# One fused attention, expert and token-mixing kernel on one core: the same instructions in another order

## The chip, the cores and the metric

The kernel runs on one core of one Trainium2 chip. The metric is the device time of one execution in microseconds (us). The kernel before took 493.33 us, the median of 3 runs (492.98 to 493.48). The engines are called as in the profile: PE (TensorE matmuls), PEld (its weight loads), DVE (VectorE), ACT (ScalarE), POOL (GpSimd), SP (the queue that issues most DMAs).

## What is computed

The reference chains three layers. Batch is 2, heads 8, sequence 768, head width 64, model width 512.

```python
q_bucket = bits of (q @ proj > 0); k_bucket likewise
mask     = q_bucket[:, :, :, None] == k_bucket[:, :, None, :]
scores   = where(mask, q @ k.T / 8, -1e9);  x = softmax(scores) @ v

for e in range(4):                      # causal attention per expert, weight of the top 2
    a = softmax(causal(x @ wq[e] @ (x @ wk[e]).T / 8)); ye = a @ (x @ wv[e]) @ wo[e]
    out += w[:, :, e] * ye

theta = x @ w_theta
y = w_tok_r @ (x * cos(theta)) + w_tok_i @ (x * sin(theta));  u = x + y
return u + relu(u @ w_ch)
```

## The kernel before

**First stage, 0 to about 240 us: hashed attention.** Sixteen heads, six row tiles of 128 queries each. A `Unit` is one such tile of a head against all 768 keys, and passes through these steps:

- `scores`: four matmuls (L986) on PE into a PSUM tile `ps`, of which there are three.
- `low`: DVE scales and masks them, with the row minimum (L1007), into the SBUF tile `T`. This frees the `ps` tile.
- `exp` on ACT (L1015).
- `flip`: DVE transposes `T` in blocks of 32 (L1022). In every second head one of the six units goes another way: six PE transposes (L1026) into a `ps` tile and a copy back on ACT (L1035).
- `mix`: when all six units of a head are flipped, a block of 96 small fp32 matmuls (L1060, two passes each, written to `ps` and to two tiles `O`) multiplies with the values `V`; six matmuls at L1068 follow in every second head. The block is held together in the order.
- `gather`, `scale`, `finish_x` on ACT, POOL and DVE end a head pair (L1095 to L1107, L906 to L913, L932).

Beside it run the preparation of later heads: `hash` (L1248, DVE L1251), `split` and `pack` (casts at L739 and L747, bit rows moved by DMA at L1262), the loads of q, k and `V` (L1134, L1140, L1151), and early parts of the later stages: expert projections (L1381, L1318), the product of two weights (`fuse_mm`, L1532, added up on DVE at L1537), and reloads of expert operands (`unstash`, L1407 and L743).

**Second stage, to about 327 us:** the causal expert attention (L1082 is its mix). **Third stage, to the end:** `theta` and `out_proj` (L1585), `trig`, `split_z`, the token mix (L1671) and the channel product (L1600).

The start of the program has a routine of its own (`first_head`): q and k of the first head arrive in pieces, on SP's queue (k, L1134) and ACT's (q, L1140), PE computes the hash bits (L1189, L1198, L1199), and DVE turns them into signs (L1211).

**What sets the order.** The program is written twice. In the first pass every job is recorded in a fixed order, which the lists `LP`, `M0`, `WT` and `VALA` place. `Plan` then replays the recording with a cost for each instruction (`price`), dependencies, PSUM and SBUF buffers, DMA lanes, and a rule for PE's own instruction fetches (`FETCH`): at each step the engine takes the ready instruction with the lowest rank. Ranks come from a backward replay; `NUDGES` then shifts some of them. In the second pass `fix` pins this order on every engine (PE, DVE, ACT, POOL and SP), and each engine works in order.

```python
        part, first, more, wake, gap, took = FETCH
...
                while count >= first + part * len(ends):
                    ends.append(max(at + wake, ends[-1] + gap if ends else 0.0) + took)
...
        for seed, a, b, ns in nudges:
            here = (rank >= a * 1e3) & (rank < b * 1e3)
            if ns < 0:
                here &= scatter(len(rank), seed + 1) > 0.85
            rank = np.where(here, rank + ns * scatter(len(rank), seed), rank)
```

## Time and profile before

| what | value |
|---|---|
| runs | 493.33 us median of 3, 492.98 to 493.48 |
| the profiled execution | 493.23 us, of which the span of the trace is 491.40 us |
| mean granted TensorE clock | 0.997 of full speed |
| busy: PE, PEld, DVE, ACT, POOL | 95%, 76%, 79%, 67%, 59% of the span |
| chain that ended last | PE 72%, DVE 10%, ACT 7%, issue 4%, POOL 3%, DMA 2% |

Busy shares are averages over stages with different limits, and a busy PE is not PE at its peak. "issue" in a chain or behind an idle time means that the engine waited for nothing that the profile names.

### The profile page before, as it was taken

The numbers are of one execution on the slowest core, as the hardware profiler recorded it, in microseconds if no ns is written. First come the engines' busy times: TensorE is split into PE (matmuls) and PEld (weight loads), VectorE is DVE, ScalarE is ACT, GpSimd is POOL, SyncE is SP. The second block draws the span as 40 slices with busy tenths as digits, with TensorE's granted clock in tenths as the row PEclk, the third lists the DMA queues.
The fourth block names the chain that finished last, engine by engine and source line by source line (L and its number), as shares of the span: only waits on it lengthen the run. The fifth ranks groups of instructions, "written<-read, shape, count | busy, mean of one in ns | idle before, by whom it ended". The sixth has DMA issues, their size and how long they took to land.

```text
span 491.4 us, 13377 instructions
## 1 busy us (share of the span) xinstructions
PE 465.1 (95%) x5360; PEld 374.0 (76%) x5360; DVE 386.3 (79%) x668; ACT 329.6 (67%) x658; POOL 288.5 (59%) x243
## 2 busy tenths in 40 slices
PE   8889988989999999898999999999999999999997
PEld 3576866677898777676789877778888888878886
DVE  6999999688894999896677684849869999676543
ACT  7788867586454978869767689997667666571110
POOL 6997999888248479226920046058557697874000
PEclk9999999899999999999999999999999999999999
DMA  7544535445785545873448324512443445470542
GB/s 245 175 140 135 162 120 157 116 149 166 195 301 174 173 151 155 232 254 108 134 150 238 99 75 134 187 38 55 145 144 131 148 151 151 109 209 34 168 145 85
DMA packets 44249, 74.17 MB, mean 151 GB/s; under 512 B 6948, under 2 KB 13892, under 8 KB 44188
## 3 DMA queue, kind: packets, MB, share of 16 engines
q1 hardware_dynamic: 42028, 69.80, 46.4%
q10 hardware_dynamic: 2160, 3.52, 1.9%
q8 instruction: 42, 0.69, 0.6%
q14 instruction: 19, 0.16, 0.1%
HBM read 54.52 MB, written 15.91 MB: 143 GB/s over the span
## 4 chain that ended last, share of the span: by engine, by line
PE 72%; DVE 10%; ACT 7%; issue 4%; POOL 3%; DMA 2%; DVEq 0%; POOLq 0%; ACTq 0%
PE ps L1671 19%; PE ps L986 9%; PE ps L1060 9%; PE ps L1381 6%; PE wk L1585 5%; DVE T L1007 5%; PE wk L1600 4%; PE O L1060 4%; PE ps L1318 4%; PE ps L1026 4%; PE O L1082 3%; PE ps L1600 3%; ACT T L1015 3%; DVE T L1022 3%; PE ps L1068 1%
## 5 line engine op out<-in xcount | busy, mean ns | idle before, releaser
L1015 ACT ACTIVATE T<-T,m 128x768 f32<-128x768 f32 (+3 forms) x144 | 121.2, 844 | 31.8 <-DVE T L1007 31.2
L1007 DVE TENSOR_SCALAR_CACHE_REDUCE T<-ps 128x768 f32<-128x768 f32 (+3 forms) x144 | 115.5, 834 | 32.2 <-PE ps L991 15.0
L1022 DVE STREAM_TRANSPOSE T<-T 128x768 f32<-128x768 f32 x88 | 82.5, 960 | 5.5 <-ACT T L1015 5.1
L1671 PE MATMUL ps<-zh,tok 128*128 128x512 f32 x240 | 76.7, 390 | 0.0
L1060 PE MATMUL ps<-T,V 32*64 32x160 f32 (+1 forms) x1536 | 63.9, 312 | 8.4 <-DVE T L1007 3.3
L1060 PE MATMUL O<-T,V 32*64 32x160 f32 (+1 forms) x1536 | 65.0, 312 | 4.8 <-issue 4.7
L1060 PEld LDWEIGHTS ps<-T,V 32*64 32x64 f32 x1536 | 54.7, 131 | 13.9 <-issue 5.2
L986 PE MATMUL ps<-op 128*128 128x512 f32 (+5 forms) x256 | 60.1, 343 | 1.1 <-DVE op L1211 0.9
L1060 PEld LDWEIGHTS O<-T,V 32*64 32x64 f32 x1536 | 50.1, 131 | 6.4 <-issue 6.3
L1671 PEld LDWEIGHTS ps<-zh,tok 128*128 128x128 f32 x240 | 45.1, 188 | 9.7
L1671 PE MATMUL ps<-zl,tok 128*128 128x512 f32 x120 | 46.3, 391 | 0.0
L802 POOL TENSOR_TENSOR tok<-raw,tok 128x512 fp32r<-128x512 f32 x27 | 41.6, 1550 | 7.9 <-PE ps L1671 4.3
L986 PEld LDWEIGHTS ps<-op 128*128 128x128 f32 (+1 forms) x256 | 39.3, 191 | 8.4 <-issue 2.7
L1035 ACT COPY T<-ps 128x768 f32<-128x768 f32 (+2 forms) x36 | 28.6, 798 | 9.0 <-PE ps L1026 8.5
L739 POOL TENSOR_SCALAR op<-op 64x768 fp32r<-64x768 f32 x8 | 6.8, 853 | 45.6 <-ACT op L1397 28.7
L1026 PE MATMUL ps<-ident,T 128*128 128x128 f32 x216 | 30.7, 277 | 1.8 <-ACT T L1015 1.1
L1107 POOL TENSOR_TENSOR ob<-ob,W 64x768 f32<-64x768 f32 x16 | 29.4, 1835 | 1.3
L1026 PEld LDWEIGHTS ps<-ident,T 128*128 128x128 f32 x216 | 23.7, 141 | 5.8 <-ACT T L1015 2.5
L1015 ACT ACTIVATION_READ_ACCUMULATOR T<-T,m 128x1 f32 x144 | 27.2, 189 | 0.0
L1671 PEld LDWEIGHTS ps<-zl,tok 128*128 128x128 f32 x120 | 22.5, 188 | 4.9
L986 PE MATMUL ps<-op,sql 128*128 128x512 f32 x84 | 24.2, 366 | 2.1 <-DVE T L1007 1.1
L1620 POOL TENSOR_TENSOR kk<-kk,x 128x512 f32<-128x512 f32 x12 | 17.8, 1482 | 13.3 <-ACT kk L1619 13.3
(236 smaller groups left out, 1161.6 us busy)
## 6 DMA issues: line engine op xcount, KB each, us to landing
V<-in_vP_dram SPq DMA_DIRECT2D x48, 256.0 KB
raw<-in_wtok_dram SPq DMA_DIRECT2D x36, 256.0 KB
raw<-tok_d SPq DMA_DIRECT2D x27, 256.0 KB
tok_d<-g SPq DMA_DIRECT2D x18, 256.0 KB
rT<-r_d SPq DMA_DIRECT2D x22, 192.0 KB
qk_d<-op SPq DMA_DIRECT2D x8, 384.0 KB
op<-qk_d SPq DMA_DIRECT2D x8, 384.0 KB
out_dram<-o ACTq DMA_DIRECT2D x11, 256.0 KB
```

What stands on the lines that cost most here:

```text
L802: nc.gpsimd.tensor_sub(l, raw, f(h))
L986: one = nc.tensor.matmul(self.sp[:, c0:c1], lhs, rhs[:, c0 - off:c1 - off], start=a == 0, stop=last)
L1007: i = nc.vector.tensor_scalar(self.ss[:, off:off + w], self.sp[:, off:off + w], -0.125, NEG, op0=OP.mult, op1=OP.min, accum_out=m)
L1015: e = nc.scalar.activation(self.ss[:, off:off + w], self.ss[:, off:off + w], AF.Exp, bias=m, scale=-1.0, accum_out=self.grp.den[:, side, i ...
L1022: nc.vector.transpose(self.ss, self.ss)
L1026: nc.tensor.transpose(self.pt[:, j * 128:(j + 1) * 128], self.P[:, j, :], ident)
L1035: nc.scalar.copy(self.P, src)
L1060: together(nc.tensor.matmul(o[a][half * 64:half * 64 + 64, 0:nb * 32], V[band, n // 4, (n - a) % 4], T[band, 0:nb, n * 32:n * 32 + 32], st ...
L1107: nc.gpsimd.tensor_add(g.ob[keep], g.ob[keep], W[keep])
L1381: nc.tensor.matmul(pp[:, c0:c1], lhs[:, kd, e, :], rhs[kd][:, c0:c1], start=n == 0, stop=n == 3 * NK - 1)
L1600: nc.tensor.matmul(o, lhs[:, sl], rhs[:, kd, cols], start=n == 0, stop=n == 3 * NK - 1)
L1671: nc.tensor.matmul(yp[t], lhs[:, a, t, :], rhs[:, a], start=i == 0 and a == 0 and n == 0, stop=i == NT - 1 and a == 1 and n == 2)
```

## The change

All of it is in the constants at the head of the file. The code, and with it every instruction, is the same.

```diff
-LP = [0, 4.5, 5.5, 2.5, 8.5, 6, 9, 13, 10, 15.0, 17.5, 15]
+LP = [0, 4.5, 5.5, 2.5, 8.5, 6, 9, 11, 10, 15.0, 17.5, 15]
-M0 = [4.5, 6, 5.5, 6, 7, 8.0, 9, 11, 11, 11, 13, 14, 12, 12, 14]
+M0 = [4.5, 6, 5.5, 6.5, 7, 8.0, 9, 11, 11, 11, 13, 14, 12, 12, 14]
-WT = [52, 51.0, 57, 52.5]
+WT = [51, 51.0, 57, 52.5]
-STAY = [[1, 4], [0, 5]]
+STAY = [[1, 4]]
-FETCH = 256, 165, 453, 1000.0, 2700.0, 1400.0
-VALA = 7.5
+FETCH = 256, 165, 453, 1000.0, 3800.0, 1400.0
+VALA = 5.5
 NUDGES = [
-    (288489, 5.7, 61.8, -1706), (998291, 190.5, 209.2, -4780), (727432, 453.6, 518.1, -1623), (283489, 92.7, 185.6, -838),
...
+    (464992, 106.3, 126.6, 867), (219712, 141.7, 161.4, -1863), (644513, 253.9, 270.5, 731), (115184, 54.4, 68.2, 800),
...
 ]
```

The table had 48 entries and has 177 now. In `FETCH` the least distance of two of PE's fetches in the replay goes from 2.7 to 3.8 us. The tile that leaves `STAY`, (0, 5), is flipped in the tail with `wide` set, where `STAY` is not asked, so this line moves nothing. The new table makes the file 31 lines longer: L1060 of the kernel before is L1091 of the changed one, and so on.

On PE 48% of the instructions stand at another place, on DVE 55%, on ACT 60%, on POOL 38%, on SP 56%, most of them by one to four places. Three places follow on which the text below rests.

**The start, on SP:** the first loads. `raw<-in_kT_dram 128x768` is k of a later head pair, `wraw` a block of the expert weights, the two first rows k of the first head. Before:

```order
L1134 DMA raw<-in_kT_dram 128x512
L1134 DMA raw<-in_kT_dram 128x256
L1151 DMA V<-in_vP_dram 128x512
L1140 DMA raw_198<-in_qT_dram 128x768
L1151 DMA V<-in_vP_dram 128x512 x2
L1134 DMA raw<-in_kT_dram 128x768
```

Now:

```order
L1165 DMA raw<-in_kT_dram 128x512
L1165 DMA raw<-in_kT_dram 128x256
L1165 DMA raw<-in_kT_dram 128x768
L878 DMA wraw<-in_wqk_dram 128x512
L1182 DMA V<-in_vP_dram 128x512
L1171 DMA raw_200<-in_qT_dram 128x768
```

The load of the later k stands directly behind the first k now, ahead of the first `V`. On DVE the small copy of `hl` (L1229, now L1260) stood between the first sign step and the next two (L1211, now L1242), and stands ahead of all three now.

**PE at 70 us of the trace:** the end of a run of `scores` (L986), the six transposes of one unit (L1026) and the first rows of a block (L1060). Before:

```order
L986 MATMUL ps<-op 128x512
L986 MATMUL ps<-op 128x256
L1026 MATMUL ps<-ident,T 128x128 x6
L1060 MATMUL ps<-T,V 64x192 x4
L1060 MATMUL O<-T,V 64x192 x4
```

Now, at the end of the same block:

```order
L1091 MATMUL ps<-T,V 64x192 x4
L1091 MATMUL O<-T,V 64x192 x4
L1017 MATMUL ps<-skh,op 128x512
L1017 MATMUL ps<-skh,op 128x256
L1057 MATMUL ps<-ident,T 128x128 x6
L1017 MATMUL ps<-skl,sqh 128x512
```

The transposes and the first `scores` of the next unit stand behind the block now, and the block follows the earlier `scores` directly. At 48 us the same exchange is made, with one unit's `scores` moved behind the block too. At 35 us and at 162 us one unit's `scores` moved from ahead of a block to behind it.

**PE and DVE at 200 us:** the last product of two weights (L1532), the `scores` of one unit (L986), a block (L1060). PE before:

```order
L1532 MATMUL ps<-wf 128x512 x6
L986 MATMUL ps<-skh,op 128x512
L986 MATMUL ps<-skh,op 128x256
L986 MATMUL ps<-skl,sqh 128x512
L986 MATMUL ps<-skl,sqh 128x256
L1060 MATMUL ps<-T,V 64x160 x4
```

Now:

```order
L1017 MATMUL ps<-skl,sqh 128x512
L1017 MATMUL ps<-skl,sqh 128x256
L1563 MATMUL ps<-wf 128x512 x6
L1091 MATMUL ps<-T,V 64x160 x4
L1091 MATMUL O<-T,V 64x160 x4
```

DVE before, with the numbers of the buffers (`low` is the row that writes `T,m`, `acc` the sum of the weight products):

```order
L1022 STREAM_TRANSPOSE T_3038<-T_3038 128x768
L1022 STREAM_TRANSPOSE T_3258<-T_3258 128x768
L1007 TENSOR_SCALAR T_3258,m_3299<-ps_3269 128x768
L1022 STREAM_TRANSPOSE T_3258<-T_3258 128x768
L1007 TENSOR_SCALAR T_3258,m_3408<-ps_3292 128x768
L1022 STREAM_TRANSPOSE T_3258<-T_3258 128x768 x2
L1537 TENSOR_TENSOR acc_2793<-ps_3281,acc_2793 128x1024
```

Now:

```order
L1053 STREAM_TRANSPOSE T_3038<-T_3038 128x768
L1038 TENSOR_SCALAR T_3262,m_3290<-ps_3265 128x768
L1053 STREAM_TRANSPOSE T_3262<-T_3262 128x768 x2
L1038 TENSOR_SCALAR T_3262,m_3408<-ps_3273 128x768
L1568 TENSOR_TENSOR acc_2802<-ps_3280,acc_2802 128x1024
L1053 STREAM_TRANSPOSE T_3262<-T_3262 128x768
L1038 TENSOR_SCALAR T_3262,m_3429<-ps_3411 128x768
```

On PE the `scores` of the unit moved behind the block, on DVE its `low` is the last row shown now, and the sum `acc` moved ahead of it.

## Rows read from the trace of the kernel before

**Rows 1.** The page: PE's instructions, its fetch queue, and the two costliest DVE groups.

```profile
PE 465.1 (95%) x5360; PEld 374.0 (76%) x5360; DVE 386.3 (79%) x668; ACT 329.6 (67%) x658; POOL 288.5 (59%) x243
...
q8 instruction: 42, 0.69, 0.6%
...
L1007 DVE TENSOR_SCALAR_CACHE_REDUCE T<-ps 128x768 f32<-128x768 f32 (+3 forms) x144 | 115.5, 834 | 32.2 <-PE ps L991 15.0
L1022 DVE STREAM_TRANSPOSE T<-T 128x768 f32<-128x768 f32 x88 | 82.5, 960 | 5.5 <-ACT T L1015 5.1
```

**Rows 2.** Stretches: length, busy PE, PEld, DVE, ACT, POOL, clock, DMA share, GB/s.

```profile
60.00:80.00 20.00, 18.60 (x377) 14.16 (x361) 19.29 (x36) 15.43 (x32) 18.62 (x18) 1.00 0.45 138
...
340.00:360.00 20.00, 20.00 (x89) 16.42 (x88) 15.88 (x17) 12.13 (x21) 14.14 (x11) 1.00 0.40 119
```

**Rows 3.** Waits of PE: in total, times, longest, in us.

```profile
PE O L1060 <- issue: 4.7, 4, 2.4
...
PE ps L1060 <- issue: 2.4, 3, 1.3
```

**Rows 4.** PE and DVE behind the pause at 82.5: timeline, and one stretch.

```profile
84.94 0.36 PE L1060 MATMUL O<-T,V 32*64 32x160 f32 x3 [2.43 <-issue]
...
85.85:89.27 3.42, 3.42 (x49) 2.56 (x36) 0.00 (x0) 1.18 (x5) 1.99 (x2) 0.50 0.71 180
...
89.83 0.96 DVE L1007 TENSOR_SCALAR_CACHE_REDUCE T<-ps 128x768 f32<-128x768 f32 x1 [4.13 <-PE ps L986]
```

**Rows 5.** DMA queues from 76.5 to 82.4 (first row) and 82.4 to 83.8.

```profile
q1 hardware_dynamic: 766, 1.61, 84.5%
...
q8 instruction: 1, 0.02, 5.4%
```

**Rows 6.** Timeline from 70 to 77: DVE, PE and SP's queue.

```profile
70.03 0.97 DVE L1022 STREAM_TRANSPOSE T<-T 128x768 f32<-128x768 f32 x1
...
72.21 0.39 PE L1060 MATMUL ps<-T,V 32*64 32x192 f32 x4 [0.94 <-DVE T L1022]
...
74.96 1.65 SPq L1151 DMA_DIRECT2D V<-in_vP_dram  x1
```

**Rows 7.** Timeline from 199 to 214: PE and DVE.

```profile
199.48 1.83 DVE L1022 STREAM_TRANSPOSE T<-T 128x768 f32<-128x768 f32 x2
...
202.22 0.36 PE L1060 MATMUL ps<-T,V 32*64 32x160 f32 x4 [1.07 <-DVE T L1007]
...
206.20 0.35 PE L1060 MATMUL ps<-T,V 32*64 32x160 f32 x2 [1.32 <-issue]
...
206.66 0.98 DVE L1022 STREAM_TRANSPOSE T<-T 128x768 f32<-128x768 f32 x1 [1.86 <-ACT T L1015]
...
213.04 0.97 DVE L1022 STREAM_TRANSPOSE T<-T 128x768 f32<-128x768 f32 x1
```

**Rows 8.** DMA queues from 197.5 to 203.5 (first row) and 203.5 to 205.

```profile
q1 hardware_dynamic: 829, 1.82, 99.7%
...
q8 instruction: 1, 0.02, 5.6%
```

**Rows 9.** The start: one stretch, and the timeline of DVE and PE.

```profile
3.00:4.00 1.00, 1.00 (x4) 0.33 (x3) 0.00 (x0) 0.54 (x2) 0.00 (x0) 1.00 1.08 381
...
6.84 0.55 DVE L1229 COPY hl<-start 128x2 f32<-128x2 f32 x1
...
8.55 0.94 PE L986 MATMUL ps<-op 76*128 76x512 f32 x4 [0.86 <-DVE op L1211]
```

**Rows 10.** Timeline of PE at three other blocks.

```profile
35.20 0.62 PE L986 MATMUL ps<-skh,op 128*128 128x512 f32 x2 [0.67 <-ACT T L1035]
...
49.86 0.39 PE L1060 MATMUL ps<-T,V 32*64 32x192 f32 x4 [0.94 <-ACT T L1035]
...
161.24 0.61 PE L986 MATMUL ps<-op,sql 128*128 128x512 f32 x2 [0.42 <-DVE op L1391]
```

**Rows 11.** Timeline of DVE in the third stage.

```profile
335.53 2.06 DVE L932 TENSOR_TENSOR y<-rT,ob 128x768 f32<-128x768 f32 x1
```

## The prediction

> **What bounds the kernel now.** I read the page first, then stretches of 20 us, then PE's waits, then timelines where PE stands. PE is busy for 95% of the span [rows 1], and in the last stretch shown it has no idle time at all, 20.00 of 20 us [rows 2]: from there to the end only less work for PE, or a new wait, can move the time. PE's idle time is 23 us in all by subtraction (491.40 less 465.1, plus what overlaps), and nearly all of it lies before 240 us, where DVE is nearly as full: 19.29 of 20 us between 60 and 80 [rows 2]. So in the first stage a wait taken from PE is worth something only if DVE is not merely late a little later; an idle time of PE that nothing on DVE causes is worth its whole length.

> There is such a kind. Seven times PE stands in the middle of a block of small matmuls with "issue" as its releaser, 7.1 us together, 2.43 the longest [rows 3, 4]. PE runs 10,720 instructions and its fetch queue moves 42 packets of 16 KB [rows 1], so one packet brings some 255 instructions, and the blocks, which are the densest code, are where PE runs out of them. The queues show why two of these pauses are long. From 76.5 to 82.4 the loads of `V` and others move 1.61 MB and no fetch packet moves; from 82.4 to 83.8 the packet comes [rows 5], and PE goes on at 84.94. From 197.5 to 203.5 it is the same with 1.82 MB at 99.7%, the packet comes behind them [rows 8], and PE stands 1.32 us, until 206.20 [rows 7]. I read this as: a fetch that is asked for while a burst of loads is under way lands when the burst is done.

> [...] Behind the pause of 1.32 us, and the shorter ones, no row shows the clock fall.

> **The change part by part.** No instruction is added or removed, so each term is a wait. The sum goes against the profiled execution, 493.23 us (491.40 of span and 1.83 around it); the median is 0.10 above, which is nothing here.

> - *Start.* PE's first scores wait 0.86 us for DVE's signs, behind which the copy of `hl`, 0.55 us, sits in DVE's row [rows 9]. As the change's order prints it, the copy comes ahead of all three sign steps, where I expect it to fall into DVE's wait for the hash bits: up to -0.77, and I take -0.5. Against it: the load of the later k, 393 KB, now stands right behind the first k, and between 3 and 4 us the queues are full (share 1.08, 381 GB/s [rows 9]). 393 KB at that rate are 1.03 us; if all of it comes ahead of the first q, that less the 0.55 is the bound, +0.5.
> - *35 us.* PE's wait of 0.67 us for a copy of ACT [rows 10] goes, and the unit moved behind the block reaches DVE later: between 0 and +0.4 (half of one `low` of 0.83 [rows 1]); I take +0.25.
> - *48 us.* The wait of 0.94 for ACT [rows 10] becomes one for the last flip: between -0.94 and 0, and -0.3 by the nearest row, one flip (0.96 [rows 1]) less the six transposes that no longer stand ahead.
> - *72 us.* The block waits 0.94 for a flip and begins at 72.21 [rows 6]. The six transposes and the next unit's scores go behind it, so it waits only for the flip begun at 70.03, which ends at 71.00: it begins some 1.16 us earlier. By itself I cost this at nothing: DVE's 19.29 of 20 us hide it, and if that cover were gone it would be a gain of up to 0.94.
> - *The fetch behind it.* The `V` loads stand on SP's queue until this block is done with its tiles (issue at 74.96 lasting 1.65 us [rows 6]), so the burst begins and ends 1.16 us earlier, and the fetch with it. The place where PE runs dry is reached at its old time, since DVE sets the pace up to there. The pause of 2.43 becomes 1.3, which is -1.17; that is below the 1.32 us after which the clock stayed up, so the 1.7 us go too: -2.9. Bounds: -2.9 and 0 (burst where it was).
> - *162 us.* Scores that waited 0.42 [rows 10] move behind the block; DVE gets them later: 0 to +0.9 (one `low`), and +0.3 taken.
> - *200 us.* The block, which waited 1.07 us for a `low` and began at 202.22, now begins at 200.45 or so: the `scores` move behind it, and it waits only for the last of the two flips from 199.48 [rows 7]. But the burst before this block is not gated by it, so the packet lands at the same time and PE stands until 206.20 again: a pause of 3.1 where there was one of 1.32, inside the same stretch. What is lost is behind it: the scores now start after the block, and their `low` comes at 208.3 where it came at 202.98, so DVE, which now waits 1.86 at 206.66 [rows 7], has five `low` (0.88 each) and three flips (0.93 to 0.97) in a row: 7.2 us, to 215.55, where the last flip of this head ended at 214.01 (213.04 and 0.97 [rows 7]). That is +1.5. Bounds: +2.4 if the clock falls behind the longer pause (half of the 1.7 of the first pause more, since about half of the stretch is this head's last block), and -0.9 if the fetch moves with the block.
> - *Third stage.* DVE's step of 2.06 us at L932 [rows 11] and two slab steps stand ahead of the first step of `theta`; PE is full there, so a wait counts whole: 0 to +0.9, +0.4 taken.
> - The other hundreds of exchanges, POOL's and SP's among them, move rows by one to four places among neighbours that wait for nothing: nothing, with the buffers between PE and DVE (three `ps` tiles) as cover; if that cover is gone at one place, one `low`, 0.83, is the price, and the range holds it.

> Sum: -0.5 +0.25 -0.3 +0 -2.9 +0.3 +1.5 +0.4 = -1.25, so 492.0 us.

> [...]

> **The rivals.**
> - *The pause at 205 takes the clock down* (0.24). The first burst isn't moved (the loads may be released by another tile of `V`), so the fetch term is 0, and the pause at 205 grows to 3.1 us. It decides at a pause as long as the one of 2.43, behind which the clock fell [rows 4]: then the 200 us term is +2.4 and the sum -0.5 +0.25 -0.3 +0.3 +2.4 +0.4 = +2.55, so 495.8 us. For it: nothing of the edit touches the loads directly. Against it: SP's queue stands exactly until the end of the block [rows 6].
> - *No change* (0.26). Fetches are late for a reason of their own, and come neither with the burst nor with the block; the pauses merely fall elsewhere with the same total. Both fetch terms are 0: -0.5 +0.25 -0.3 +0.3 +0.4 = +0.15, 493.4 us. For it: there are seven pauses [rows 3], and I found such a burst ahead of two. Against it: no packet of the fetch queue in 1.61 MB of others [rows 5]. [...]
> - *Both bursts move* (0.12). At 200 the loads of `V` come ahead of a waiting row on SP's queue and are done early, the packet too: the 200 us term is -0.9, less one third for what DVE then sets (-0.6), and the sum -3.35, so 489.9 us.

> **How the numbers follow.** The forecast, 492.0 us, has 0.38. A measurement here tells from no change what is over 0.2%, 1.0 us. Of the forecast's 0.38 I count 0.30 as faster (it lies 1.3 below the median), 0.06 within and 0.02 above. Of "no change" 0.04, 0.18 and 0.04; of the slow rival 0.05 within and 0.19 slower; the fast one is all faster. Together faster 0.46, the same 0.29, slower 0.25. The range, 489.4 to 495.4, takes in the fast rival and leaves out the slow rival's upper half and small tails, under 0.2. The forecast's own range is 490.8 to 493.2.

> **What would show it right or wrong.** In the changed kernel's trace: the block at 72 begins near 71, the load of `V` is issued about 1.2 us earlier, the pause behind it is about 1.3 us and no stretch near 86 has a clock of 0.50. At 200 the block begins over 1 us earlier and stands about 3 us; its head's last flip ends 1.5 us later against the kernel's other marks. The first scores start near 8 us. PE stays at 20.00 of 20 from 340 on, with at most one new wait near 335. The forecast falls if the pause near 82 is still over 2 us, if the clock falls anywhere new, or if seven pauses of another place and length add to the same 7 us.

## The result and the profile after

The changed kernel takes 498.05 us (median of 6 runs, 497.09 to 500.0), the kernel before 493.38 (median of 6 on the same chip): a ratio of 1.0101, with a 95% interval of 1.0077 to 1.0125. It is slower by 1.0%, where 492.0 was forecast; the time lies above the range, and above the slow rival's 495.8. A second set of runs on another chip gave 1.0103 (1.0065 to 1.0142). On the chips of the later sets the runs of the kernel before spread from 489.3 to 499.5, so every ratio below is to the kernel before on its own chip. One profile (of the first run of the exchange undone, 567.4 us at a mean clock of 0.755) was taken from a disturbed execution and isn't read.

The page of the changed kernel, profiled in an execution of 497.28 us (span 495.5): busy times, and PE's two groups of the block, whose fields behind the second bar are the idle time before them and what ended most of it.

```profile
PE 469.0 (95%) x5360; PEld 377.0 (76%) x5360; DVE 383.7 (77%) x668; ACT 328.6 (66%) x658; POOL 286.0 (58%) x243
...
L1091 PE MATMUL O<-T,V 32*64 32x160 f32 (+1 forms) x1536 | 65.5, 314 | 8.1 <-issue 8.1
L1091 PE MATMUL ps<-T,V 32*64 32x160 f32 (+1 forms) x1536 | 64.5, 313 | 5.1 <-DVE T L1038 1.9
```

PE's waits for its own instructions (total, times, longest):

```profile
PE O L1091 <- issue: 8.1, 6, 4.5
...
PE ps L1091 <- issue: 1.9, 3, 1.0
...
PE ps L1099 <- issue: 1.5, 1, 1.5
```

Against 7.1 us in 7 waits [rows 3] these are 11.5 us in 10, the longest 4.5 us in place of 2.4. Yet all idle time of PE up to its last instruction is about the same (23.4 us against 23.2): the waits for other engines fell by what the waits for instructions rose. PE's busy time rose by 3.9 us, for the same instructions. Of that some 2.5 us are a slower clock, by an estimate: PE worked 8.42 us at a clock of 0.50 here, against 3.41 before [rows 4], and half of the difference is counted as lost. The other 1.3 us lie mostly in the scores (L1017), and no run shows what made them longer. The stretches say where the clock was slow. Of 200 to 220 us first the kernel before, then the changed one, and in it the stretch at a clock of 0.50:

```profile
200.00:220.00 20.00, 16.62 (x436) 13.41 (x435) 17.53 (x30) 13.67 (x32) 4.32 (x4) 1.00 0.77 240
```

```profile
200.00:220.00 20.00, 14.59 (x244) 11.43 (x239) 12.07 (x21) 9.23 (x19) 4.33 (x4) 0.74 0.60 177
204.14:214.38 10.24, 8.42 (x79) 6.73 (x79) 3.20 (x6) 2.33 (x7) 1.68 (x3) 0.50 0.53 154
```

For 10.24 us the clock is 0.50, and PE is busy for 8.42 of them, which costs some 4.2 us. That is an estimate, half of the 8.42: rows of four of the block's matmuls on `ps` began every 0.27 us there (206.57 to 207.37) and every 0.14 us at a clock of 1.00 (200.30 to 200.98). Here DVE is busy for 12.07 us where it was for 17.53.

### The profile page after: what moved, and what is told of

It is laid out like the page before. It is cut to its first block, busy times and chain, and to the rows that moved or that the text cites. A ratio compares the mean times of both kernels' runs of the same rounds, so it can differ in the third digit from the quotient of the medians.

```text
span 495.5 us, 13363 instructions
## 1 busy us (share of the span) xinstructions
PE 469.0 (95%) x5360; PEld 377.0 (76%) x5360; DVE 383.7 (77%) x668; ACT 328.6 (66%) x658; POOL 286.0 (58%) x243
## 4 chain that ended last, share of the span: by engine, by line
PE 73%; DVE 9%; ACT 6%; issue 5%; POOL 4%; DMA 3%; SPq 0%; DVEq 0%; POOLq 0%; ACTq 0%
PE ps L1702 20%; PE ps L1017 10%; PE ps L1091 7%; PE ps L1412 6%; PE wk L1616 6%; DVE T L1038 4%; PE wk L1631 4%; PE ps L1349 4%; PE ps L1057 3%; PE O L1091 3%; PE ps L1631 3%; PE O L1113 3%; DVE T L1053 3%; ACT T L1046 2%; ACT op L778 1%
## 5 line engine op out<-in xcount | busy, mean ns | idle before, releaser
L1046 ACT ACTIVATE T<-T,m 128x768 f32<-128x768 f32 (+4 forms) x144 | 121.3, 844 | 36.1 <-DVE T L1038 35.6
L1053 DVE STREAM_TRANSPOSE T<-T 128x768 f32<-128x768 f32 x88 | 82.4, 960 | 4.0 <-ACT T L1046 3.8
L1702 PE MATMUL ps<-zh,tok 128*128 128x512 f32 x240 | 75.5, 390 | 0.0
L1091 PE MATMUL O<-T,V 32*64 32x160 f32 (+1 forms) x1536 | 65.5, 314 | 8.1 <-issue 8.1
L1091 PE MATMUL ps<-T,V 32*64 32x160 f32 (+1 forms) x1536 | 64.5, 313 | 5.1 <-DVE T L1038 1.9
L1091 PEld LDWEIGHTS ps<-T,V 32*64 32x64 f32 x1536 | 55.2, 132 | 10.5 <-DVE T L1038 4.5
L1017 PE MATMUL ps<-op 76*128 76x256 f32 (+5 forms) x256 | 62.5, 345 | 0.6 <-DVE op L1242 0.5
L1091 PEld LDWEIGHTS O<-T,V 32*64 32x64 f32 x1536 | 50.3, 132 | 10.1 <-issue 10.0
L1017 PEld LDWEIGHTS ps<-op 128*128 128x128 f32 (+1 forms) x256 | 40.3, 192 | 6.6 <-DVE op L1242 0.5
L1057 PE MATMUL ps<-ident,T 128*128 128x128 f32 x216 | 32.7, 277 | 1.0 <-ACT T L1046 0.7
L1017 PE MATMUL ps<-skh,op 128*128 128x512 f32 x84 | 25.2, 376 | 1.6 <-ACT W L1126 0.9
L1017 PE MATMUL ps<-op,sql 128*128 128x512 f32 x84 | 24.6, 370 | 2.1 <-DVE T L1038 1.5
```

What stands on the lines that cost most here:

```text
L1017: one = nc.tensor.matmul(self.sp[:, c0:c1], lhs, rhs[:, c0 - off:c1 - off], start=a == 0, stop=last)
L1046: e = nc.scalar.activation(self.ss[:, off:off + w], self.ss[:, off:off + w], AF.Exp, bias=m, scale=-1.0, accum_out=self.grp.den[:, side, i ...
L1053: nc.vector.transpose(self.ss, self.ss)
L1057: nc.tensor.transpose(self.pt[:, j * 128:(j + 1) * 128], self.P[:, j, :], ident)
L1091: together(nc.tensor.matmul(o[a][half * 64:half * 64 + 64, 0:nb * 32], V[band, n // 4, (n - a) % 4], T[band, 0:nb, n * 32:n * 32 + 32], st ...
L1702: nc.tensor.matmul(yp[t], lhs[:, a, t, :], rhs[:, a], start=i == 0 and a == 0 and n == 0, stop=i == NT - 1 and a == 1 and n == 2)
```

## Where the time went

The same places of PE's program in the two traces, from timelines (L1060 is L1091 now; the end is that of L1600, now L1631):

| place on PE | before, us | changed, us | difference |
|---|---|---|---|
| first block begins | 25.27 | 25.20 | -0.06 |
| block at 50 ends | 54.56 | 52.66 | -1.90 |
| next block begins | 58.29 | 58.19 | -0.11 |
| block at 72 ends | 76.37 | 75.74 | -0.63 |
| block at 97 ends | 101.92 | 100.00 | -1.92 |
| block at 190 ends | 194.40 | 192.34 | -2.06 |
| block at 200 begins | 202.22 | 198.76 | -3.46 |
| it goes on after its pause | 206.20 | 205.96 | -0.24 |
| it ends | 207.53 | 208.36 | +0.84 |
| next block begins | 214.11 | 218.62 | +4.50 |
| second stage begins | 236.54 | 240.58 | +4.04 |
| it ends | 326.57 | 330.02 | +3.45 |
| end | 488.29 | 492.32 | +4.03 |

So the changed kernel was 2.06 us ahead at 192 us, and lost 6.6 us between there and 219. Behind that the difference only wanders, by 1 us. The timeline of PE and DVE at that place:

```profile
198.76 0.36 PE L1091 MATMUL ps<-T,V 32*64 32x160 f32 x4 [0.38 <-DVE T L1038]
...
205.96 0.54 PE L1091 MATMUL O<-T,V 32*64 32x160 f32 x3 [4.51 <-issue]
...
209.98 0.96 DVE L1038 TENSOR_SCALAR_CACHE_REDUCE T<-ps 128x768 f32<-128x768 f32 x1 [6.64 <-PE ps L1017]
```

The block began 3.46 us earlier and then stood for 4.51 us, so that it went on at nearly the same time as before [rows 7]. The queues, from 197.5 to 203.5 and from 203.5 to 204.7:

```profile
q1 hardware_dynamic: 771, 1.61, 95.4%
...
q8 instruction: 1, 0.02, 5.7%
```

Again no packet of PE's fetch queue comes in a full stretch of loads, and one comes right after it, as in [rows 8]. What the block had gained stood still; 2.7 us into the standstill the clock fell, and the scores behind the block, on which DVE waited 6.64 us, ran at a clock of 0.50: a pair of them took 0.64 us (209.10 to 209.74) where the same pair took 0.36 at 1.00 (194.03 to 194.39).

That PE went on at 205.96 where it did at 206.20 before is a coincidence, and not a fixed time of landing. The loads come with PE: in the changed kernel SP issues the first `V` load 0.2 us after the block at 190 ends (192.34), before the change 0.95 us after it (194.40). First the kernel before, then the changed one:

```profile
195.35 0.98 SPq L1151 DMA_DIRECT2D V<-in_vP_dram  x2
```

```profile
192.53 0.98 SPq L1182 DMA_DIRECT2D V<-in_vP_dram  x2
```

So the block at 190 is the mark to count from. Before, PE ran out of instructions 10.48 us behind it and the packet began at 9.20; in the changed kernel PE ran out at 9.10 and the packet began at 11.22, behind six loads of `V` and 2.58 MB where there were five and 2.12. The pause grew at both ends, by 1.4 us and by 1.8, and the lead of 2.06 us hid the second.

That these pauses come at a fixed place in PE's own instructions can be counted. In the thirteen profiles read here, 58 waits of PE's matmuls over 0.7 us have "issue" as their releaser, ten of them in the kernel before and the changed one (0.71 to 4.51 us). With PE's matmuls, weight loads and semaphore waits numbered from 0 in the order of each trace, the matmul that ends such a wait has always the number 193 or 194, counted modulo 256.

## The experiments

**Theory.** A packet of PE's instructions that is asked for in a burst of loads lands only behind it; the order lets the block run out of instructions sooner against these loads and so makes the pause longer; and the clock that falls behind the long pause makes up most of the 4.7 us. **Rival 1:** the packet is late for a reason of its own. **Rival 2:** the clock falls for another reason than the pause.

The experiments change the order alone, by one line behind the replay: the named instructions stand right behind another on their engine. (In the excerpts below the table `BEHIND` is shown without the `NUDGES = [` that follows on its line.)

```diff
-t, order, reuse = plan.arrange(SLACK, 6, NUDGES)
+t, order, reuse = plan.arrange(SLACK, 6, NUDGES); order = {e: [m for n in r if n not in sum(BEHIND.values(), []) for m in [n] + BEHIND.get(n, [])] for e, r in order.items()}
```

`BEHIND` names instructions by their number in the recording. The three runs that move the scores also exchange the slots of two PSUM tiles (`reuse = [(old, SLOTS.get(new, new)) for old, new in reuse]`), so that the block or the scores don't wait for the other's tile.

**The burst taken away at 200 us, in the changed kernel.** The six loads of `V` go behind the block (three behind a load at 205, three behind one at 214):

```diff
+BEHIND = {2506: [2362, 2361, 2360], 3238: [2553, 2552, 2554]}
```

> The changed kernel with its six loads of V from 192.5 to 197.6 us moved on SP's queue to behind the block at 200 us. Theory (a late packet of PE's instructions stops the block, since it lands only when the burst of loads is done, and the long pause takes the clock down): the packet that landed at 203.55 lands before 201.4, there is no pause near 201, the clock stays 1.00 from 200 to 220, and the time falls by the 6.6 us that the block and what follows it lose there, to 491.5 (490.7 to 492.5). Rival 1 (the packet comes late for a reason of its own): it still lands near 203.5, pause 4 to 4.5 us, time 497.5 to 498.5. Rival 2 (the clock falls for another reason than the pause): no pause, but a clock of 0.50 in 200 to 220, time 494 to 496.

Measured: 1.0008 of the kernel before (0.9979 to 1.0038; median 493.52 of 12 runs). The profile, the block's pause and the stretch, and two stretches near the start:

```profile
203.88 0.36 PE L1091 MATMUL O<-T,V 32*64 32x160 f32 x3 [1.11 <-issue]
```

```profile
200.00:220.00 20.00, 15.98 (x431) 12.96 (x431) 17.61 (x33) 12.27 (x28) 4.26 (x4) 1.00 0.74 253
21.80:28.63 6.83, 6.64 (x106) 5.28 (x112) 6.83 (x14) 5.84 (x12) 6.50 (x7) 0.50 0.09 19
49.11:52.52 3.41, 3.41 (x96) 3.41 (x89) 3.38 (x8) 2.56 (x5) 3.33 (x4) 0.50 0.18 50
```

The packet began 7.6 us after the end of the block at 190, in the changed kernel 11.2 us; the pause is 1.11 in place of 4.51, the clock 1.00, DVE's work 17.61 us as before the change. Both rivals fall for this place. The time came back by 0.9%, 4.6 us of 4.7, and not to the 491.5 expected (6.6 us). In this profile the clock fell twice near the start instead (mean clock 0.990), but the runs with a mean clock of 0.996 or 0.997 took 491.0 to 493.8 too, so these falls aren't shown to be what is missing.

**The exchange alone, in the kernel before,** with the burst and without it. Scores of one unit go behind the block, and their `low` behind the sum of the weight products; the second run also moves the five loads of `V` at 195 to 200 us:

```diff
+BEHIND = {2831: [2847, 2848, 2849, 2850], 2727: [2852]}; SLOTS = {'ps_3406': 'ps_3289', 'ps_3289': 'ps_3406'}
```

```diff
+BEHIND = {2831: [2847, 2848, 2849, 2850], 2727: [2852], 2506: [2361, 2360], 3238: [2554, 2553, 2552]}; SLOTS = {'ps_3406': 'ps_3289', 'ps_3289': 'ps_3406'}
```

> The kernel before with that one exchange alone (scores of one unit behind the block at 200 us, DVE's row for it behind the sum of the weight products, the two score tiles' slots exchanged). Theory: the block begins near 200.5, pauses some 3 us until 206.2, the clock falls to 0.50 for several us, DVE waits for scores for over 4 us, and the time rises by 3 to 5 us to 496.5 to 498.5. Rival 2 (the clock falls for another reason): pause 3 us without a fall, 494.5 to 495.3. Rival 1: 493 to 494.

> The kernel before with the exchange at 200 us alone, as in the run that took 1.011 of it, and with its five loads of V at 195 to 200 us moved. Theory (the exchange costs only because the packet lands behind the loads): the pause near 203 is under 1.5 us, no fall of the clock at 200 to 220, and the time is 0.997 to 1.003 of the kernel before. Rival (the exchange itself starves DVE): 1.006 to 1.012 still.

Measured: the exchange with the burst 1.0110 (1.0062 to 1.0158; median 497.86), without it 1.0008 (0.9976 to 1.0040; 492.94). The block's pause with the burst, DVE behind it, and the lower clock:

```profile
209.82 0.54 PE L1060 MATMUL O<-T,V 32*64 32x160 f32 x4 [3.77 <-issue]
...
213.84 0.96 DVE L1007 TENSOR_SCALAR_CACHE_REDUCE T<-ps 128x768 f32<-128x768 f32 x1 [3.19 <-PE ps L986]
...
209.24:216.07 6.83, 6.25 (x75) 4.86 (x75) 2.54 (x5) 1.23 (x4) 0.83 (x1) 0.50 0.68 223
```

and without the burst:

```profile
202.54 0.36 PE L1060 MATMUL O<-T,V 32*64 32x160 f32 x4 [0.76 <-issue]
...
200.00:220.00 20.00, 16.75 (x406) 13.13 (x390) 16.64 (x29) 12.68 (x30) 3.54 (x4) 1.00 0.75 249
```

One exchange among the hundreds costs about as much as the whole change, but only while the loads are in front of the packet. That is the cause, shown in both kernels. Its size is known less well: the six runs with the burst lie between 493.56 and 500.81, and the profile is of the slowest, which has a second loss that isn't the exchange's, a pause of 3.24 us at 86.7 and 6.83 us of the lower clock there. From the end of the block at 190 to the start of the block behind the one at 200 it took 4.5 us more than the kernel before (24.17 against 19.71).

**The exchange undone, in the changed kernel,** in two sets:

```diff
+BEHIND = {2726: [2847, 2848, 2849, 2850]}; SLOTS = {'ps_3406': 'ps_3289', 'ps_3289': 'ps_3406'}
```

> The changed kernel with one exchange on PE undone: the scores of one unit stand ahead of the block at 200 us again, and the two score tiles take their slots as before. Theory: the block begins 1.4 to 2 us later, PE runs dry at about 203, the packet still lands near 203.5, the pause is 1.5 to 2.2 us, the clock stays up, and the time is 491.5 to 492.5. If a pause of this length is enough for the clock to fall: 494 to 495. Rival 1 (the loss at 200 has nothing to do with where the block stands): 497.5 to 498.5.

> The same kernel as a_x once more (one exchange at 200 us undone), since that run's profile had a clock of 0.75 throughout and says nothing of the stages; its times were 498. Theory: the block begins at 200 to 201 us and stands for 2 to 2.5 us before the packet that lands near 203.5; the clock falls behind that pause for 3 to 7 us, as behind the 2.28 us pause of the kernel with the loads at 75 moved, and the time is 495 to 498.5. Rival (the loss has nothing to do with the pause): no fall and a pause under 1.5 us, yet 498.

Measured: 1.0112 (1.0063 to 1.0161; median 498.16 of the other 5 runs), then 1.0044 (1.0008 to 1.0080; median 494.38 of 10). The first expectation missed, with a time in the range of its rival. The second had 2 to 2.5 us for the pause and 495 at the least, and was just missed too. The second profile shows why the exchange undone isn't a cure:

```profile
203.17 0.36 PE L1091 MATMUL ps<-T,V 32*64 32x160 f32 x4 [1.64 <-DVE T L1038]
...
207.76 0.29 PE L1091 MATMUL ps<-T,V 32*64 32x160 f32 x1 [1.92 <-issue]
...
208.94:215.76 6.82, 6.82 (x33) 5.38 (x28) 2.71 (x5) 3.54 (x9) 2.66 (x2) 0.50 0.75 247
```

PE now stands 1.64 us for DVE ahead of the block and 1.92 in it, and the clock falls behind the two. The packet still began 11.2 us after the end of the block at 190. With the burst in front, PE stands either way: ahead of the block for the scores' `low`, or in it for the packet. This profile, too, is of the slowest run, and has a fall of 6.83 us at 66, behind a pause of 2.85, long before the exchange.

**Half of the burst,** three of the six loads moved:

```diff
+BEHIND = {3238: [2553, 2552, 2554]}
```

> The changed kernel with three of its six loads of V at 192 to 197 us moved (786 KB, about 1.8 us of the 3.6 us by which six loads brought the packet forward). Theory: against the block's own place the packet lands 1.5 to 2.2 us sooner than in the changed kernel, the pause is 2.2 to 3.2 us, the clock still falls behind it, for 3 to 7 us, and the time lies between the changed kernel's and that with six moved: 1.003 to 1.008 of the kernel before. Rival (the packet's time is not set by the amount of the loads): pause as in the changed kernel, or none.

Measured: 1.0003 (0.9969 to 1.0036; 489.1 to 498.1 in 12 runs). The packet began 9.3 us after the end of the block at 190, 1.9 us sooner than with all six and 1.7 later than with none: its time follows the amount of the loads, as expected. The pause is as expected too, but in this profile no fall follows it:

```profile
205.02 0.36 PE L1091 MATMUL O<-T,V 32*64 32x160 f32 x3 [2.90 <-issue]
...
205.10:211.00 5.90, 5.67 (x84) 4.40 (x84) 3.74 (x7) 3.26 (x10) 1.85 (x3) 1.00 0.86 250
```

So the expected 1.003 to 1.008 failed with the fall it counted on.

**A standstill of another kind.** With the six loads moved, the flip that the block waits for goes five rows later on DVE:

```diff
+BEHIND = {2506: [2362, 2361, 2360], 3238: [2553, 2552, 2554], 2851: [2718]}
```

> The changed kernel with its six loads of V moved (so its instructions are there) and, on DVE, the flip that the block at 200 us waits for put five rows later: PE waits some 5 us for DVE there in place of instructions. Theory (any standstill of that length takes the clock down, whatever PE waits for): one wait of 4 to 5.5 us on DVE near 200, then a clock of 0.50 for 6 to 11 us, and the time 4 to 8 us over the same kernel without that row moved. Rival (only a standstill inside a block, for want of instructions, does that): the wait, no fall, 3 to 5 us over it.

```profile
208.36 0.54 PE L1091 MATMUL ps<-T,V 32*64 32x160 f32 x4 [5.20 <-DVE T L1053]
...
207.64:211.06 3.42, 2.70 (x81) 2.73 (x89) 0.57 (x1) 0.00 (x0) 0.83 (x1) 0.50 1.03 285
```

The clock fell 4.5 us into a wait for DVE, for 3.41 us where 6 to 11 were expected, but without any lack of instructions. So here the fall came with neither a block under way nor a late packet. The time, 501.5 in one execution, can't be set against the others, as the same profile has two more falls, of 6.83 us each, behind pauses of 2.37 and 2.24 us at 62 and 86.

**The burst at 75 us, in the kernel before:** three loads behind one at 87.7; then also the five at 195 to 200. The 1.7 us in both expectations is half of the 3.42 us busy at 0.50 [rows 4], an estimate.

```diff
+BEHIND = {1377: [899, 900, 898]}
```

```diff
+BEHIND = {1377: [899, 900, 898], 2506: [2361, 2360], 3238: [2554, 2553, 2552]}
```

> The kernel before with the three loads of V at 75 to 78 us moved on SP's queue to behind the load at 87.7 us. Theory: the packet that landed at 83.7 lands before 81.5, the pause of 2.43 us goes, the clock stays 1.00 from 85 to 90, and the time falls by up to 2.43 + 1.7 = 4.1 us, less what DVE then sets: 489.3 to 491.5. Rival 1 (the packet is late for a reason of its own): pause and clock as before, 493 to 494.

> The kernel before with the three loads of V at 75 us and the five at 195 to 200 us moved to behind the blocks. Theory: neither pause is over 1.3 us, the clock stays 1.00 from 5 us on, and the time is 2.4 + 1.7 + 0.7 us or so under the kernel before, less 1 us for DVE: 488.5 to 490.5. Rival (the packets' lateness moves elsewhere, behind the later loads): the sum of the pauses stays at 6 to 7 us, 491.5 to 493.5.

Measured: 0.9980 (0.9951 to 1.0008) and 1.0004 (0.9967 to 1.0040): neither can be told from the kernel before. In the first profile the pause at 82 went from 2.43 to 0.77 and the fall at 86 is gone, though the packet began at 82.15, later than expected and 0.3 us earlier than before: PE came there 1.1 us later. The block at 200 stood longer, and the clock fell there:

```profile
84.39 0.36 PE L1060 MATMUL O<-T,V 32*64 32x160 f32 x3 [0.77 <-issue]
...
205.69 0.35 PE L1060 MATMUL ps<-T,V 32*64 32x160 f32 x2 [2.28 <-issue]
...
206.01:209.43 3.42, 3.42 (x72) 2.65 (x56) 2.02 (x3) 0.54 (x4) 0.83 (x1) 0.50 0.95 323
```

In the second, with both bursts moved, the loads stood in front of the next packet: from 206.5 to 212.7 us the queues moved 2.52 MB and no fetch packet, and the block there paused 2.86 us, with a fall behind it (mean clock of the execution 0.997). That is the rival named in its expectation, and the theory's mechanism at another place.

```profile
q1 hardware_dynamic: 1239, 2.52, 104.9%
...
215.30 0.37 PE L1060 MATMUL O<-T,V 32*64 32x192 f32 x1 [2.86 <-issue]
```

**More loads moved, in the changed kernel:** the six and the three at 75; then also the three at 55 us, which stand ahead of the pause of 1.47 us at 63 that the kernel before has not.

```diff
+BEHIND = {1377: [898, 899, 900], 2506: [2362, 2361, 2360], 3238: [2553, 2552, 2554]}
```

```diff
+BEHIND = {719: [553, 551, 552], 1377: [898, 899, 900], 2506: [2362, 2361, 2360], 3238: [2553, 2552, 2554]}
```

> The changed kernel with the six loads at 192 to 197 us and the three at 75 us moved behind the blocks. Theory: no pause over 1.6 us and no fall of the clock at 85 to 90 or 200 to 220; as the changed kernel was 2 us ahead at 200 us, 488 to 490.5, the fastest of all, if the start is undisturbed (falls at 22 and 49 us as in the run with six loads moved would add 3 to 5 us). Rival (what it gained to 200 us was the shorter pause at 83 alone): the same as the kernel before with both groups moved.

> The changed kernel with twelve loads of V moved behind blocks: the three at 55 us, the three at 75 us and the six at 192 to 197 us. Theory: the pauses at 62, 84 and 201 us are each under 1.3 us, most runs have a mean clock of 0.997 or more, and the median is under the kernel before: 0.994 to 0.999 of it. Rival (other waits take their place, the clock falls elsewhere): 1.000 to 1.004, as with nine moved.

Measured: nine loads 1.0023 (0.9985 to 1.0061; median 493.01, where 488 to 490.5 was expected: the rival's case), twelve 0.9932 (0.9898 to 0.9967; median 489.97 of 12 runs, 486.93 the lowest). The second is **faster than both kernels**, by 0.7% than the one before and by 1.7% than the change; this is a little more gain than the 0.994 to 0.999 expected, with a mean clock of 0.997 or more in six of the twelve runs and not in most. The profile with nine has no fall from 5.8 us to the end and took 490.29 us, but its other runs had mean clocks down to 0.985, and its pause at 63 was 1.69 us here, and 1.36 to 2.85 in the other profiles of this order. With twelve that pause is gone:

```profile
PE O L1091 <- issue: 4.2, 5, 1.3
PE ps L1091 <- issue: 3.6, 3, 2.1
```

7.8 us in 8 waits, with one of 2.1 us left, in the block at 213, behind which this profile has its one fall within the work (215.08 to 218.50, clock 0.50).

**The changed kernel once more,** beside three of these on their chip:

> The changed kernel as it is, beside the others on one chip. Theory (the loss is the clock behind the long pause at 201 us): 1.006 to 1.014 of the kernel before, the pause near 201 over 3.5 us again, the clock 0.50 behind it for over 6 us, and a mean clock under 0.99 in nearly every run.

Measured: 1.0103 (1.0065 to 1.0142), pause 4.53 us near 206, clock 0.50 behind it for 3.41 us, and for 6.83 us more at 87, behind a pause of 2.99 us. The place is the same, and how long the clock stays down is not: the expectation had over 6 us. The changed kernel was not ahead in this profile: the block at 190 ended at 196.41, 2.0 us later than in the kernel before, and PE stood as long as when it was 2.06 us ahead. So the pause doesn't come of the lead. The mean clock of the six runs is 0.987 (0.985 to 0.990), of the 29 runs of the kernel before on that chip 0.994, of the twelve with twelve loads moved 0.996. From the means, the changed kernel spends 2 x 0.013 x 496 = 13 us at a clock of 0.50 and the kernel before 5.5 us, an estimate; if PE does half the work in them, up to 3.7 of the 5.1 us between their means are the clock.

**The place at 200 us in all of these,** counted in us from the end of the block at 190; the last column is the start of the block behind:

| kernel | `V` loads ahead of the packet | packet begins | PE runs out | pause | lower clock at the place | block behind |
|---|---|---|---|---|---|---|
| before | 5 | 9.20 | 10.48 | 1.32 | 0 | 19.71 |
| changed | 6 | 11.22 | 9.10 | 4.51 | 10.24 | 26.28 |
| changed, once more | 6 | 11.22 | 9.11 | 4.53 | 3.41 | 24.64 |
| before, exchange alone | 5 | 10.14 | 8.86 | 3.77 | 6.83 | 24.17 |
| changed, exchange undone | 6 | 11.23 | 11.70 | 1.92 | 6.83 | 24.80 |
| changed, three loads moved | 3 | 9.32 | 9.10 | 2.90 | 0 | 21.41 |
| changed, six moved | 0 | 7.59 | 9.09 | 1.11 | 0 | 19.61 |
| before, exchange and five moved | 0 | 7.31 | 8.86 | 0.76 | 0 | 19.75 |

## Why the prediction was wrong

The step that failed is the term of **200 us**, by its size: +1.5, with +2.4 at most, against the 6.6 us measured. The sum's other parts were nearer: up to 192 us it had -3.15 and 2.06 were gained, behind the place +0.4, and 0.5 were gained there. That the block would begin early and stand long was right, and so was that PE would go on near 206.20 (205.96), but this last by luck. Two things were mis-sized. First, the pause, 3.1 forecast and 4.51 measured. The term had the packet land at its old time, since the burst isn't gated by this block. But the burst follows the block at 190 (the table above), and against that block the packet came 2.0 us later than before; in the profile of the result the lead of 2.06 us cancels that, in the second profile, 2.0 us behind, it doesn't, and the pause is the same. The term also set its times against the old trace and left out the lead that the sum itself had by then. Second, the clock: the rival put its fall at half of the 1.7 us of the other pause, 0.9; it lasted 10.24 us with 8.42 us of work, some 4.2 us (in the second profile 3.41 us, 1.7).

The rival "the pause at 205 takes the clock down" named the mechanism and its place, and came to 495.8 because of these two sizes, and because it was tied to a first burst that doesn't move.

The **fetch** term, -2.9, was right in its sign in the profile of the result and wrong in its cause. The pause did shrink, to 1.05, and the clock stayed up; in the second profile of the same kernel it was 2.99 us and the clock fell behind it for 6.83, so this gain isn't a steady one. But the burst did not end sooner: 1.75 MB moved from 76.5 to 82.4 us (1.61 before [rows 5]) and the packet began at 82.55 (82.48). PE came there later, held 0.94 us by ACT at 77.30 and for some more by its instructions, so the lead rose from 0.63 to 1.92, by 1.3 and not 2.9:

```profile
78.24 0.50 PE L1017 MATMUL ps<-skh,op 128*128 128x512 f32 x1 [0.94 <-ACT W L1126]
...
85.16 0.35 PE L1091 MATMUL O<-T,V 32*64 32x160 f32 x2 [1.05 <-issue]
```

No run shows the 1.7 us that this term, and by half the bound at 200 us, take for the clock: they are an estimate, half of the 3.42 us busy at 0.50 [rows 4]. In their place the profile of the result shows a clock of 1.00 from 85.85 to 89.27, and in it rows of four of the block's matmuls began every 0.27 us at 0.50 and every 0.14 at 1.00, and a pair of the scores took 0.64 and 0.36.

The **start** gave -0.06 at the first block where -0.5 was taken: PE's wait of 0.86 shrank to 0.25, but the matmuls ahead of it ended later, and the first scores began at 8.66 where they had begun at 8.55. At **35** and **48** the block ended 1.0 and 1.9 us early, more than the terms, and all but 0.11 was gone at the next block, since DVE set the pace; the sum of the two, -0.05, was about right there. At **72** the wait of 0.94 for a flip became 0.78 for a `low`: the block began 0.63 us earlier, half of what was read from the order. **162** gave no loss: the lead was 2.49 us at the block's end and 1.59 at the block before it. The **third stage** was to cost 0.4 and cost 0.6: +3.45 at its front and +4.03 at the end. One reading was wrong without harm: 491.40 less 465.1 is 26.3 and not 23; 3.2 of it lie behind PE's last instruction at 488.29.

Under a burst a packet let PE stand for up to 4.53 us in these profiles, and its delay went from 11.2 to 9.3 to 7.6 us as three and six loads were moved. No run shows when PE asks for the packet, or where it waits in between.

## What to carry to other kernels

When an order brings a dense block forward, look at what the block still waits for that isn't in the order: here its own instructions, which came behind the loads under way (11.2 us after the block ahead with six loads, 7.6 with none). Ask what starts those loads: here the end of the block ahead, so a kernel that is early brings them along and its pause stays, and a pause at an old place on the clock proves nothing. A long standstill of the tensor engine was paid twice in most of these traces, in the wait and in the clock behind it (4.51 us, and then 10.24 at 0.50, in the changed kernel). So loads that aren't urgent are best kept out of the way of the packet: the new order showed a gain only once twelve loads of 256 KB had moved (0.7% under the kernel before), and eight moved in the old order showed none. Twelve moved in the old order weren't run, so whether the gain is the order's or the loads' stays open.
